# A fused attention and expert kernel: the fourth expert's first product on the second part by seven products of halves, and the float64 weights converted through DRAM

## The chip, the cores and the metric

The kernel runs on one core of a Trainium2 chip. The metric is the device time of one execution, in microseconds (us). Engines: PE multiplies matrices (PEld loads its weights), DVE and ACT work elementwise, POOL stands beside them, and SP issues the DMAs. Each engine runs its own instructions in order and waits for the others through semaphores.

## The reference

```python
x = attention(q, k, v)              # 2304 rows of 512
p = domain_probs / sum(domain_probs)
for e in range(4):                  # w1[e] 512 x 1024, w2[e] 1024 x 512
    h = maximum(x @ w1[e], 0)
    out += p[:, e] * (h @ w2[e])
h = out @ w_in                      # 512 x 1024, given as float64
ln = layernorm(h * softmax(h)) * g_ln
return ln @ w_out                   # 1024 x 512, given as float64
```

## The kernel before, in words

Every operand of a product is held as two float16 parts, a high and a low one, and every product is the sum of three: high by high, high by low, low by high. The 2304 rows are 18 tiles of 128. Tiles 0 to 5 are part 0 and tiles 6 to 17 are part 1; part 1 is four groups of three tiles (384 rows). A phase is one expert on one part: `j` 0 to 3 are the experts on part 0 (interleaved with the attention), `j` 4 to 7 the same experts on part 1. In the trace phases 6 and 7, the third and the fourth expert on part 1, stand from 685 to 802 us and from 802 to 928 us, and then the second layer follows (L1283 on).

A group of a phase has two halves. The **first product** is x by w1. In phases 4 and 7 it is the ordinary one (`phase_units`, `emit_h`): 8 column blocks of 12 matmuls of 384 columns, and for each block ACT writes the high part of relu(h) into a tile `hch` (L319) and DVE the low part (L320). In phases 5 and 6 it is made by seven products of halves (`st_phase`, `st_units`): x is cut into four quarters (two halves of its rows, two of the summed dimension), w1 likewise, and seven products of sums of quarters replace eight. The sums of x, `T`, are made once for each group (`t_steps`), those of w1, `S`, once for each expert and column half (`s_steps`, on DVE and ACT, in buffers `stf` and `stl`). A group has two column halves, each with seven products of 12 matmuls of 192 columns (L529). DVE joins their results: seven additions a column half (`add`, L541, tiles `stu`), which read the products from PSUM; ACT copies the first product (L559), and of each of four results ACT and DVE write high and low parts (L547, L548, two each). The products take turns in five PSUM banks, so PE can be at most five products ahead of the DVE addition that reads them.

The **second product**, `out_unit`, is 24 matmuls of 512 columns for each of the three tiles of a group (L331), and one DVE instruction adds it to `acc` (L355). For the last expert `finish_x2` scales, splits and transposes the finished tile for the second layer.

Weights: `next_w` hands out the steps of one matrix: four loads of 512 KB into `stage`, a scale, and four splits into the high and low parts `wt` (L263 on ACT, L266 on DVE). There is one `stage` buffer, so the next matrix can be loaded when the last L266 of the one before has read it. The two float64 matrices have another first step (`load64` and `to32`): 1024 KB are loaded, and seven DVE instructions on 1024 elements (L189 to L213) turn the two 32-bit words of a number into a float32 in `stage`. Before the change both matrices are converted so in phase 7.

`spread` puts such steps between the units of a phase, and a list scheduler of the framework then sets the order in which each engine gets its instructions; `high_priority` puts the evictions first. Memory comes from pools; a tile with one buffer (`bufs=1`) waits until the readers of the one before it are done, and a pool that takes the place of another waits for the readers of that.

Of the kernel before, what the change touches and what calls it, by code (L numbers as in the profile page):

```python
# [58 lines left out]
def tile_kernel(  # L59
# [101 lines left out]
    def w_steps(key, src, bits, inv, tag, load_eng, rows=None, hi_eng=None, place_raw="stage", known=False):  # L161
# [5 lines left out]
        wide = src.dtype == I64  # L167
        raw = {}

        def load64(c):  # L170
            def f():
                r = cv["pool"].tile([128, 1024, 2], I32, tag="raw64", name="raw64")
                dv = src.bitcast(I32).rearrange("(k p) f -> p k f", p=128)
                load_eng.dma_start(
                    out=r.rearrange("p (k f) w -> p k (f w)", k=q), in_=dv[:, c * q:(c + 1) * q]
                )
                raw[c] = r
            return f

        def to32(c):  # L180

            a = [None, None]

            def words():
                r = raw[c]
                a[0] = cv["pool"].tile([128, 1024], I32, tag="cvA", name="cvA")
                a[1] = cv["pool"].tile([128, 1024], I32, tag="cvP", name="cvP")
                h = r[:, :, 1]
                vec.tensor_scalar(  # L189
                    out=a[0], in0=h, scalar1=3, scalar2=0x3FFFFFF8,  # L190
                    op0=ALU.logical_shift_left, op1=ALU.bitwise_and,
                )
                vec.scalar_tensor_tensor(
                    out=a[0], in0=h, scalar=-0x40000000, in1=a[0], op0=ALU.bitwise_and, op1=ALU.bitwise_or
                )
                vec.tensor_scalar(
                    out=a[1], in0=h, scalar1=0x7FFFFFFF, scalar2=None, op0=ALU.bitwise_and
                )

            def value():  # L200
                top, tmp = a[0].bitcast(F32), a[1].bitcast(F32)
                vec.scalar_tensor_tensor(
                    out=top, in0=a[1], scalar=float(896 << 20), in1=top, op0=ALU.is_ge, op1=ALU.mult
                )
                vec.tensor_scalar(
                    out=a[1], in0=a[0], scalar1=-0x800000, scalar2=None, op0=ALU.bitwise_and
                )
                o = stage[key][:, c * 1024:(c + 1) * 1024]
                vec.scalar_tensor_tensor(
                    out=o, in0=raw.pop(c)[:, :, 0].bitcast(U32), scalar=2.0 ** -52, in1=tmp,  # L210
                    op0=ALU.mult, op1=ALU.mult,
                )
                vec.tensor_tensor(out=o, in0=o, in1=top, op=ALU.add)  # L213

            return [words, value]

# [59 lines left out]
        if wide:  # L276
            steps = [load64(0), load64(1), load]
            for c in range(4):
                steps += to32(c)
                if c < 2:  # L280
                    steps.append(load64(c + 2))
# [327 lines left out]
    def next_w(hi_eng=None, eng=None, place_raw="stage"):  # L609
# [4 lines left out]
        if i == 16:  # L614
            return w_steps("w_in", w_in, 15, inv, tag, eng)
# [816 lines left out]
```

## Time and profile before

| | us |
|---|---|
| median of 3 runs (lowest to highest) | 1121.17 (1119.93 to 1123.97) |
| the profiled execution | 1120.33 |
| its span | 1118.5 |
| PE busy in the span | 1054.0 |
| DVE busy in the span | 821.9 |
| ACT busy in the span | 500.8 |

The span lies within the profiled execution's time; 1.8 us lie around it. Matmuls overlap in the pipeline, as do instructions of DVE: what one costs its engine is the distance from its start to the next start, and not the duration that stands beside it.

### The profile page before, as it was taken

How to read it: one execution, taken by the hardware profiler on the slowest of the kernel's cores; microseconds unless marked ns; L12 is line 12 of the kernel's file. 1: busy time of each engine (PE TensorE's matmuls, PEld its weight loads, DVE VectorE, ACT ScalarE, POOL GpSimd, SP SyncE). 2: the span in 40 equal slices, each digit the busy share in tenths (PEclk: the TensorE clock that was granted, in tenths of full speed). 3: DMA queues.
4: the chain of work that ended last, by engine and by line, in shares of the span. 5: the costliest groups of instructions: out<-in, count | busy, mean ns of one | idle time of the engine just before them, and what ended most of it. 6: DMA issues, size and time to landing. Idle time of an engine off the chain costs nothing.

```text
span 1118.5 us, 19987 instructions
## 1 busy us (share of the span) xinstructions
PE 1054.0 (94%) x7776; PEld 642.1 (57%) x7776; DVE 821.9 (73%) x1818; ACT 500.8 (45%) x1115; POOL 184.7 (17%) x176
## 2 busy tenths in 40 slices
PE   4479889899998999999999999999999999999998
PEld 4456766466565555655567777766555554444443
DVE  6888787648678678536997459544999656999883
ACT  5657676647655457433542224211324332333222
POOL 4874632323115411000000000000000000000000
PEclk9999999899999999999999999999999999999999
DMA  9868986837648748332150002200422101443343
GB/s 306 236 149 176 248 183 148 246 94 209 174 103 236 152 114 224 74 43 56 33 203 6 1 1 79 73 1 1 148 87 96 38 19 29 89 90 85 76 85 85
DMA packets 216063, 125.87 MB, mean 113 GB/s; under 512 B 183712, under 2 KB 185760, under 8 KB 215456
## 3 DMA queue, kind: packets, MB, share of 16 engines
q1 hardware_dynamic: 215968, 124.59, 43.4%
q8 instruction: 61, 1.00, 0.4%
q14 instruction: 34, 0.28, 0.1%
HBM read 73.18 MB, written 6.29 MB: 71 GB/s over the span
## 4 chain that ended last, share of the span: by engine, by line
PE 73%; DVE 11%; DMA 8%; POOL 4%; issue 3%; ACT 1%; SPq 0%; DVEq 0%; ACTq 0%; POOLq 0%
PE ops L331 27%; PE hps L311 15%; PE hps L529 9%; PE h L1283 8%; PE o L1346 8%; DMA pT<-hl 6%; PE pv L872 3%; DVE wt L266 2%; DVE hl L843 1%; PE sps L799 1%; PE sps L800 1%; DVE stf L437 1%; DMA vraw<-in_vC_dram 1%; POOL wt L259 1%; DVE hch L320 1%
## 5 line engine op out<-in xcount | busy, mean ns | idle before, releaser
L331 PE MATMUL ops<-wt,hch 128*128 128x512 f16 x1728 | 387.6, 379 | 3.9 <-DVE wt L266 1.6
L331 PEld LDWEIGHTS <-hch 128*128 128x128 f16 x1728 | 166.2, 98 | 190.4 <-issue 4.4
L311 PE MATMUL hps<-xT,wt 128*128 128x384 f16 (+1 forms) x1920 | 268.5, 297 | 1.7 <-DVE hch L320 1.3
L311 PEld LDWEIGHTS <-wt 128*128 128x128 f16 x1920 | 164.0, 100 | 85.9 <-issue 4.0
L838 ACT ACTIVATE p<-sps,nm 128x320 f32<-128x320 f32 (+4 forms) x144 | 79.1, 553 | 89.9 <-DVE nm L809 59.6
L843 DVE TENSOR_TENSOR hl<-p,hl 128x320 f16<-128x320 f32 (+4 forms) x132 | 90.5, 699 | 33.2 <-ACT hl L842 32.9
L266 DVE SCALAR_TENSOR_TENSOR wt<-stage,ws,wt 128x1024 f16<-128x1024 f32 x72 | 99.7, 1392 | 8.3 <-ACT wt L263 6.9
L355 DVE SCALAR_TENSOR_TENSOR acc<-ops,coef,acc 128x512 f32<-128x512 f32 x54 | 40.4, 748 | 82.1 <-PE ops L331 82.1
L1283 PE MATMUL h<-wt,x2T 128*128 128x512 f16 x432 | 95.5, 379 | 0.8 <-DVE acc L355 0.8
L319 ACT ACTIVATE hch<-hps 128x384 f16<-128x384 f32 x130 | 62.3, 482 | 75.1 <-PE hps L311 74.6
L1346 PE MATMUL o<-wt,lt 128*128 128x512 f16 x432 | 95.5, 379 | 0.0
L320 DVE SCALAR_TENSOR_TENSOR hch<-hps,hch 128x384 f16<-128x384 f32 x130 | 70.5, 544 | 32.2 <-ACT hch L319 32.2
L799 PE MATMUL sps<-ks,qhi 128*128 128x288 f32 (+3 forms) x160 | 67.4, 424 | 23.7 <-ACT p L838 10.1
L263 ACT ACTIVATE wt<-stage,ws 128x1024 f16<-128x1024 f32 x64 | 71.1, 1140 | 6.0 <-PE hps L311 2.2
L1283 PEld LDWEIGHTS <-x2T 128*128 128x128 f16 x432 | 42.2, 98 | 52.0 <-issue 1.1
L541 DVE TENSOR_TENSOR stu<-stu,hps 128x384 f32<-128x384 f32 x112 | 59.4, 550 | 17.3 <-PE hps L529 17.3
L1346 PEld LDWEIGHTS <-lt 128*128 128x128 f16 x432 | 42.3, 98 | 50.9
L547 ACT ACTIVATE hch<-stu 128x192 f16<-128x192 f32 x128 | 39.2, 354 | 70.4 <-DVE stu L541 70.2
L842 ACT ACTIVATE hl<-p 128x320 f16<-128x320 f32 (+4 forms) x132 | 66.0, 522 | 7.3 <-DMA pT<-hl 6.7
L872 PE MATMUL pv<-v,pT 128*128 128x64 f16 x1392 | 54.8, 197 | 13.6 <-DMA pT<-hl 13.6
L529 PEld LDWEIGHTS <-S 128*128 128x128 f16 x768 | 64.3, 98 | 2.6
L872 PEld LDWEIGHTS <-pT 128*128 128x128 f16 x1392 | 49.4, 101 | 22.6 <-DMA pT<-hl 17.5
(155 smaller groups left out, 1366.7 us busy)
## 6 DMA issues: line engine op xcount, KB each, us to landing
stage<-in_w_dram SPq DMA_DIRECT2D x64, 512.0 KB, 5.9
raw<-in_qT_dram SPq DMA_DIRECT2D x34, 256.0 KB, 3.5
vraw<-in_vC_dram SPq DMA_DIRECT2D x30, 256.0 KB, 3.3
raw<-in_kT_dram SPq DMA_DIRECT2D x24, 288.0 KB, 3.5
raw<-in_w_in_dram SPq DMA_DIRECT2D x4, 1024.0 KB, 4.8
raw<-in_w_out_dram SPq DMA_DIRECT2D x4, 1024.0 KB, 5.0
out_dram<-o2s SPq DMA_DIRECT2D x16, 256.0 KB, 2.5
raw<-in_kT_dram SPq DMA_DIRECT2D x8, 192.0 KB, 4.1
```

Of the source, the lines that this page charges most:

```text
L263: h = bg_(act.activation(out=hi, in_=r, func=AF.Copy, scale=stage[key, "s"]), "A")
L266: stage["last"] = vec.scalar_tensor_tensor(out=lo, in0=r, scalar=stage[key, "s"], in1=hi, op0=ALU.mult, op1=ALU.subtract)
L311: pe.matmul(ps[:, j * n:j * n + n], w[:, a, kk, f * 128:(f + 1) * 128], x[:, b * KD + kk, c0:c0 + n], start=(m == 0), stop=(m == 3 * KD - 1),)
L320: nc.vector.scalar_tensor_tensor(out=h[:, 1, :n], in0=ps[:, :n], scalar=0.0, in1=h[:, 0, :n], op0=ALU.max, op1=ALU.subtract)
L331: pe.matmul(ps, hch[f][:, a, o0:o0 + 128], w[:, b, f, :], start=(m == 0), stop=(m == 3 * KF - 1))
L529: pe.matmul(ps[c][:, jj * HT:jj * HT + HT], lhs(a, kk, jj), rhs(b, kk), start=(m == 0), stop=(m == 5),)
L799: pe.matmul(o, hi[:, h % 4], rhs, start=True, stop=False)
L838: act.activation(out=dst, in_=src, func=AF.Exp, bias=nm[:, j + x:j + x + 1], scale=SCALE, accum_out=sums[:, h:h + 1],)
L843: anc["D"] = vec.tensor_tensor(out=hl[:, W + c0:W + c0 + n_], in0=pf[:, 0:n_], in1=hl[:, c0:c0 + n_], op=ALU.subtract)
L872: pe.matmul(o, tt[:, a * nch + c, :], v[:, bb, hs], start=(m == 0), stop=(m == total - 1))
L1283: pe.matmul(ps[:, half], x[:, a * KD + kk, c:c + 128], w[:, b, kk, half * 512:half * 512 + 512], start=(m == 0), stop=(m == 3 * KD - 1),)
L1346: pe.matmul(ps, tt[:, a * KF + f], w[:, b, f], start=(m == 0), stop=(m == 3 * KF - 1))
```

## The change

Phase 7 takes the form of phases 5 and 6: its first product is made by seven products of halves. For that its `S` is made at the end of phase 6, as that of phase 6 is made at the end of phase 5. The conversion of the float64 matrices is taken out of `w_steps`. It works on pieces of 512 elements, eight for each matrix: load the words (512 KB), seven DVE instructions, store the float32 piece (256 KB) to a DRAM tile `w32`. `w_in` is converted in phase 6 and `w_out` in phase 7, and then each is loaded from `w32` into `stage` as the other matrices are. The piece's DVE buffers `cvA` and `cvP` have one buffer each, its words two. The pool `tmp` of the sums and the pool `cv` of the conversion take each other's place (`swap`), and the tiles `stu` have a pool of their own with fewer buffers.

```diff
+    def to32_steps(src, tag):
+        n, W = src.shape[1], 512
+        d = dp.tile([src.shape[0], n], F32, tag=tag, name="w32")
...
+            def load():
+                a[2] = st_["cv"].tile([128, W, 2], I32, tag="raw64", name="raw64", bufs=2)
+                sync.dma_start(out=a[2].rearrange("p f w -> p (f w)"), in_=sv[:, k, 2 * f:2 * f + 2 * W])
+            def words():
+                a[0] = st_["cv"].tile([128, W], I32, tag="cvA", name="cvA")
+                a[1] = st_["cv"].tile([128, W], I32, tag="cvP", name="cvP")
...
+            def value():
...
+                vec.tensor_tensor(out=o, in0=o, in1=top, op=ALU.add)
+                sync.dma_start(out=dv[:, k, f:f + W], in_=o)
+            return [load, words, value]
...
+    def swap(name):
+        if "es" in st_:
+            st_["es"].close()
+        st_["es"] = ExitStack()
+        if name:
+            st_[name] = st_["es"].enter_context(tc.tile_pool(name=name, bufs=1))
...
         def add(k, x, y):
-            n = {"s": 3, "u": 2}.get(k[0], 1)
-            u[k] = st_["tmp"].tile([128, W], F32, tag=k[0] + str(n), name="stu", bufs=n)
+            n = 2 if k[0] == "s" else 1
+            u[k] = st_["acc"].tile([128, W], F32, tag=k[0] + str(n), name="stu", bufs=n)
...
-    for j in (5, 6):
+    for j in (5, 6, 7):
...
+        if j < 7:
...
+            end = [s_steps(e + 1, h) for h in range(2)]
...
+        elif j == 6:
+            swap("cv")
+            st = to32(0)
+            n = len(st) // 3
+            tasks = [tasks[0] + st[:n], tasks[1] + st[n:2 * n], st[2 * n:], pb + [lambda: swap("tmp")]]
+        else:
+            swap("cv")
+            st = to32(1)
+            n = len(st) // 2
+            pa, qa = next_w()
+            pb, qb = next_w()
+            tasks = [post + st[:n] + pa[:5], st[n:] + pa[5:] + qa, pb[:5], (pb[5:], qb)]
...
-    us = phase_units(7, GROUPS[1], psb)
```

Two places on DVE. The lines of the changed file are others: there the additions are L556, the low parts L563, the weight splits L216, the additions to `acc` L362, the conversion L251 to L274 and the scaling of rows of `w_out` L186.

First, DVE at the start of phase 6, behind the last addition to `acc` of phase 5. Before:

```order
L266 SCALAR_TENSOR_TENSOR wt_9521<-stage_9268,ws_9270,wt_9521 128x1024
L541 TENSOR_TENSOR stu_9125<-stu_9109,hps_9112 128x384
L541 TENSOR_TENSOR stu_9131<-stu_9075,hps_9112 128x384
L266 SCALAR_TENSOR_TENSOR wt_9521<-stage_9268,ws_9270,wt_9521 128x1024
L541 TENSOR_TENSOR stu_9146<-stu_9109,hps_9133 128x384
L266 SCALAR_TENSOR_TENSOR wt_9521<-stage_9268,ws_9270,wt_9521 128x1024
L548 SCALAR_TENSOR_TENSOR hch_9045<-stu_9125,hch_9045 128x192
L541 TENSOR_TENSOR stu_9167<-stu_9131,hps_9154 128x384
```

The same place in the changed kernel, DVE:

```order
L556 TENSOR_TENSOR stu_9158<-stu_9118,hps_9145 128x384
L216 SCALAR_TENSOR_TENSOR wt_9498<-stage_9187,ws_9189,wt_9498 128x1024
L251 TENSOR_SCALAR cvA_9307<-raw64_9263 128x512
L258 TENSOR_SCALAR cvP_9308<-raw64_9263 128x512
L216 SCALAR_TENSOR_TENSOR wt_9498<-stage_9187,ws_9189,wt_9498 128x1024
L563 SCALAR_TENSOR_TENSOR hch_9053<-stu_9135,hch_9053 128x192
L563 SCALAR_TENSOR_TENSOR hch_9054<-stu_9135,hch_9054 128x192
L563 SCALAR_TENSOR_TENSOR hch_9053<-stu_9158,hch_9053 128x192
L563 SCALAR_TENSOR_TENSOR hch_9054<-stu_9158,hch_9054 128x192
L255 SCALAR_TENSOR_TENSOR cvA_9307<-raw64_9263,cvA_9307 128x512
L216 SCALAR_TENSOR_TENSOR wt_9498<-stage_9187,ws_9189,wt_9498 128x1024
L556 TENSOR_TENSOR stu_9224<-stu_9208,hps_9211 128x384
```

Behind it come `stu_9181<-stu_9141,hps_9168`, which is what `stu_9167<-stu_9131,hps_9154` is before, and the fourth split. Three conversion instructions and three more low parts have moved ahead of it.

Second, DVE in phase 7 between the second products of its second group and the first product of its third, where the rows of `w_out` are scaled by `g_ln`. Before:

```order
L213 TENSOR_TENSOR stage_10865<-stage_10865,cvA_10988 128x1024
L236 TENSOR_SCALAR stage_10865<-stage_10865,gl_94 128x512 x4
L189 TENSOR_SCALAR cvA_11031<-raw64_10950 128x1024
L196 TENSOR_SCALAR cvP_11032<-raw64_10950 128x1024
L355 SCALAR_TENSOR_TENSOR acc_6808<-ops_10868,coef_10576,acc_6808 128x512
L193 SCALAR_TENSOR_TENSOR cvA_11031<-raw64_10950,cvA_11031 128x1024
```

The same place in the changed kernel, DVE:

```order
L216 SCALAR_TENSOR_TENSOR wt_11318<-stage_10878,ws_10880,wt_11318 128x1024
L362 SCALAR_TENSOR_TENSOR acc_6808<-ops_11319,coef_10881,acc_6808 128x512
L264 SCALAR_TENSOR_TENSOR cvA_11123<-cvP_11124,cvA_11123 128x512
L362 SCALAR_TENSOR_TENSOR acc_6852<-ops_11358,coef_10881,acc_6852 128x512
L267 TENSOR_SCALAR cvP_11124<-cvA_11123 128x512
L131 TENSOR_SCALAR x2i_95<-xt_11345 128x1
L270 SCALAR_TENSOR_TENSOR cvP_11124<-raw64_11054,cvP_11124 128x512
L135 TENSOR_SCALAR x2i_95<-x2i_95 128x1
L186 TENSOR_SCALAR stage_11525<-stage_11525,gl_94 128x512
L131 TENSOR_SCALAR x2i_95<-xt_11384 128x1
L186 TENSOR_SCALAR stage_11525<-stage_11525,gl_94 128x512
L274 TENSOR_TENSOR cvP_11124<-cvP_11124,cvA_11123 128x512
```

The last split of `w_in` (the first row) has moved close ahead of the first L186, whose `stage` now comes by a load that may begin only when that split has read the buffer; before, DVE itself had written it.

## Rows read from the trace of the kernel before

**Rows 1.** PE timeline, groups of phases 6 and 7: start, us, engine, line.
```profile
743.56 1.15 PE L529 MATMUL hps<-xT,wt 128*128 128x192 f16 x12
...
757.42 15.70 PE L331 MATMUL ops<-wt,hch 128*128 128x512 f16 x72
...
802.36 15.76 PE L311 MATMUL hps<-xT,wt 128*128 128x384 f16 x96
817.96 15.70 PE L331 MATMUL ops<-wt,hch 128*128 128x512 f16 x72
```

**Rows 2.** All instructions of line 529: duration ns min/median/max.
```profile
L529 PEld LDWEIGHTS <-S x768: 97/98/98, 542.6 to 786.7; 128*128 128x128 f16 x192
```

**Rows 3.** Windows: length, busy us of PE, PEld, DVE, ACT, POOL; clock, DMA.
```profile
685.00:802.00 117.00, 117.00 (x933) 81.53 (x932) 73.34 (x154) 31.98 (x81) 0.00 (x0) 1.00 0.13 47
802.00:928.00 126.00, 125.35 (x679) 66.26 (x678) 94.67 (x167) 47.42 (x89) 0.00 (x0) 1.00 0.25 73
```

**Rows 4.** DVE timeline, start of phase 6 and a stretch of phase 7.
```profile
687.26 0.74 DVE L355 SCALAR_TENSOR_TENSOR acc<-ops,coef,acc 128x512 f32<-128x512 f32 x1
687.92 0.62 DVE L548 SCALAR_TENSOR_TENSOR hch<-stu,hch 128x192 f16<-128x192 f32 x2
688.46 0.69 DVE L425 TENSOR_TENSOR S<-stf,S 128x512 f16<-128x512 f32 x1
689.06 0.75 DVE L355 SCALAR_TENSOR_TENSOR acc<-ops,coef,acc 128x512 f32<-128x512 f32 x1
...
695.43 0.55 DVE L541 TENSOR_TENSOR stu<-stu,hps 128x384 f32<-128x384 f32 x1
695.90 0.35 DVE L548 SCALAR_TENSOR_TENSOR hch<-stu,hch 128x192 f16<-128x192 f32 x1
696.16 1.28 DVE L266 SCALAR_TENSOR_TENSOR wt<-stage,ws,wt 128x1024 f16<-128x1024 f32 x1
697.36 0.55 DVE L541 TENSOR_TENSOR stu<-stu,hps 128x384 f32<-128x384 f32 x1
...
808.97 0.68 DVE L189 TENSOR_SCALAR cvA<-raw 128x1024 int32<-128x1024 int32 x1
809.57 0.69 DVE L196 TENSOR_SCALAR cvP<-raw 128x1024 int32<-128x1024 int32 x1
...
810.64 1.21 DVE L193 SCALAR_TENSOR_TENSOR cvA<-raw,cvA 128x1024 int32<-128x1024 int32 x1
811.78 0.54 DVE L320 SCALAR_TENSOR_TENSOR hch<-hps,hch 128x384 f16<-128x384 f32 x1
...
875.23 0.48 DVE L236 TENSOR_SCALAR stage<-stage,gl 128x512 f32<-128x512 f32 x1
875.62 0.15 DVE L135 TENSOR_SCALAR x2i<-x2i 128x1 f32<-128x1 f32 x1
```

**Rows 5.** PE timeline, the first products of phase 6.
```profile
695.95 2.14 PE L529 MATMUL hps<-T,S 128*128 128x192 f16 x24
```

**Rows 6.** DMA issues by line: KB each, median us from issue to landing.
```profile
spill<-acc SPq DMA_DIRECT2D x6, 256.0 KB, 2.0
```

**Rows 7.** DMAs into `stage` from 685 to 702 us: four in a row.
```profile
DMA to landing us min/median/max: 4.2/5.6/6.5
```

**Rows 8.** PE timeline: its waits, in brackets what ended them.
```profile
122.42 1.78 PE L872 MATMUL pv<-v,pT 128*128 128x64 f16 x30 [2.24 <-DMA pT<-hl]
580.45 1.15 PE L529 MATMUL hps<-T,wt 128*128 128x192 f16 x12 [1.62 <-DVE stu L541]
928.20 2.10 PE L1283 MATMUL h<-wt,x2T 128*128 128x512 f16 x9 [0.84 <-DVE acc L355]
```

**Rows 9.** Windows at the first and the second of these waits, same columns as above.
```profile
120.00:133.10 13.10, 10.86 (x109) 7.58 (x106) 7.49 (x14) 8.35 (x19) 6.72 (x7) 0.87 1.04 243
...
123.00:124.00 1.00, 1.00 (x23) 1.00 (x21) 0.00 (x0) 0.87 (x3) 0.82 (x2) 0.50 0.97 323
...
568.00:626.00 58.00, 56.23 (x447) 38.83 (x446) 40.47 (x88) 17.34 (x44) 0.00 (x0) 1.00 0.19 69
```

More of the change, by code (lines that the diff above doesn't have):

```diff
@@ L165, in w_steps @@
         q = k // 4
[L167 to L215, printed above, removed]
         def load():
@@ L275, in w_steps @@
         steps = [load] + [load_part(c) for c in range(4)]
[L276 to L281, printed above, removed]
         if rows is not None:
@@ L286, in w_steps, with piece @@
         return steps, [place] + [split(c) for c in range(4)]
+    def to32_steps(src, tag):
+        n, W = src.shape[1], 512
+        d = dp.tile([src.shape[0], n], F32, tag=tag, name="w32")
+        sv = src.bitcast(I32).rearrange("(k p) f -> p k f", p=128)
+        dv = d.rearrange("(k p) f -> p k f", p=128)
+        steps = []
+        def piece(k, f):
+            a = [None, None, None]
+            def load():
[4 more added lines that the diff above has]
+                a[1] = st_["cv"].tile([128, W], I32, tag="cvP", name="cvP")
+                h = a[2][:, :, 1]
+                vec.tensor_scalar(
+                    out=a[0], in0=h, scalar1=3, scalar2=0x3FFFFFF8,
+                    op0=ALU.logical_shift_left, op1=ALU.bitwise_and,
+                )
+                vec.scalar_tensor_tensor(
+                    out=a[0], in0=h, scalar=-0x40000000, in1=a[0], op0=ALU.bitwise_and, op1=ALU.bitwise_or
+                )
+                vec.tensor_scalar(
+                    out=a[1], in0=h, scalar1=0x7FFFFFFF, scalar2=None, op0=ALU.bitwise_and
+                )
+            def value():
+                top, o = a[0].bitcast(F32), a[1].bitcast(F32)
+                vec.scalar_tensor_tensor(
+                    out=top, in0=a[1], scalar=float(896 << 20), in1=top, op0=ALU.is_ge, op1=ALU.mult
+                )
+                vec.tensor_scalar(
+                    out=a[1], in0=a[0], scalar1=-0x800000, scalar2=None, op0=ALU.bitwise_and
+                )
+                vec.scalar_tensor_tensor(
+                    out=o, in0=a[2][:, :, 0].bitcast(U32), scalar=2.0 ** -52, in1=o,
+                    op0=ALU.mult, op1=ALU.mult,
+                )
+                vec.tensor_tensor(out=o, in0=o, in1=top, op=ALU.add)
+                sync.dma_start(out=dv[:, k, f:f + W], in_=o)
+            return [load, words, value]
+        ps = [piece(k, f) for k in range(src.shape[0] // 128) for f in range(0, n, W)]
+        steps = [ps[0].pop(0)]
+        for a, b in zip(ps, ps[1:] + [[]]):
+            steps += b[:1] + a
+            del b[:1]
+        return d, steps
@@ L289, in tile_kernel, with to32 @@
+    last_w = [w_in, w_out]
+    def to32(i):
+        if last_w[i].dtype != I64:
+            return []
+        last_w[i], steps = to32_steps(last_w[i], f"w32{i}")
+        return steps
     xT, x2T, acc = {}, {}, {}
@@ L556, in f1 @@
             product(1, A(0, 0), B(0, 0))
-            u["b"] = st_["tmp"].tile([128, W], F32, tag="b1", name="stu", bufs=1)
+            u["b"] = st_["acc"].tile([128, W], F32, tag="b1", name="stu", bufs=1)
             with tc.high_priority(offset=PRI):
@@ L601, in st_phase @@
             else:
-                gs = spread(gs + outs, (1, n + 3, tasks[g]))
+                if isinstance(tasks[g], tuple):
+                    gs = spread(gs + outs, (1, n, tasks[g][0]), (n + 0.2, n + 2.5, tasks[g][1]))
+                else:
+                    gs = spread(gs + outs, (1, n + 2.5, tasks[g]))
             us += gs
@@ L614, in next_w @@
         if i == 16:
-            return w_steps("w_in", w_in, 15, inv, tag, eng)
+            return w_steps("w_in", last_w[0], 15, inv, tag, eng)
         if i == 17:
-            return w_steps("w_out", w_out, 15, inv, tag, eng, rows=gl)
+            return w_steps("w_out", last_w[1], 15, inv, tag, eng, rows=gl)
         j, second = divmod(i, 2)
@@ L1227, in tile_kernel @@
     st_["keep"] = sts.enter_context(tc.tile_pool(name="keep", bufs=1))
-    st_["tmp"] = sts.enter_context(tc.tile_pool(name="tmp", bufs=2))
+    st_["acc"] = sts.enter_context(tc.tile_pool(name="sacc", bufs=1))
+    swap("tmp")
     moe.reverse()
```

25 lines of the change are left out of this document (8 added, 17 removed).

## The prediction

> **What bounds the kernel now.** I read the PE timeline of phases 6 and 7 first. A group of phase 6 spends 757.42 − 743.56 = 13.86 us on its first product and a group of phase 7 spends 817.96 − 802.36 = 15.60 us; the second product, 72 matmuls, follows without a gap in both [rows 1]. The reader should see that the two kinds of group differ in the first product alone. The windows come next: in phases 6 and 7 PE is busy for 117.00 of 117 and 125.35 of 126 us at a clock of 1.00 (2.4 GHz), DVE for 73.34 and 94.67 us, ACT for 31.98 and 47.42 us [rows 3]. So PE sets the time there, and the engine to watch is DVE, because the change gives it work. The third view is DVE's own timeline, for what an instruction costs it: the distance between two starts, not the duration beside it [rows 4].
>
> **What PE saves.** Four groups of phase 7 take the form of phase 6: 4 × (15.60 − 13.86) = 6.96 us less, if PE doesn't wait. A matmul of 192 columns then costs 13.86 / 168 = 82.5 ns, one of 384 columns 15.60 / 96 = 162.5 ns. The form has 168 weight loads a group in place of 96, each recorded with 98 ns [rows 2], and yet the matmuls start 82.5 ns apart: the loads overlap. The Trainium skill speaks against the form here (TensorE: Matmul & The Clock Gate, LDWEIGHTS): a weight load takes its columns divided by 1.2, in ns. By that, as an estimate, 128 columns need 107 ns, a group would take 168 × 0.107 = 17.9 us, and the change would cost 9 us where the rows give a gain of 7. The trace has this very instruction stream in phase 6 and differs from it, and the trace decides.
>
> **What DVE gets.** Prices from start to start [rows 4]: an addition of 384 elements 695.90 − 695.43 = 0.47 us; a low part (687.92 to 688.46, two of them) 0.27; 512 elements of two tensors 0.60 (688.46 to 689.06); an addition to `acc` 0.66; a weight split 1.20; a TENSOR_SCALAR of 1024 elements 0.60 and the three-operand form 1.14 (810.64 to 811.78); a scaled row of `stage` 0.39. For 512 elements of the conversion the trace has no row. I bound a TENSOR_SCALAR by half of 0.60 and by the 0.39 of the scaled row and take 0.35; I bound the three-operand form by 0.60 and 0.66 and take 0.63.
> - Phase 7: 56 additions × 0.47 + 64 low parts × 0.27 = 43.6 us, in place of 32 × 0.47 = 15.0 us for L320: +28.6 us.
> - `S` of the fourth expert: 14 instructions a half, 28 × 0.60 = +16.8 us, in phase 6.
> - Conversion: a piece is 3 × 0.35 + 3 × 0.63 + 0.60 = 3.5 us, sixteen are 57 us. Before, eight of 3 × 0.60 + 4 × 1.14 = 6.4 us are 51 us: +6 us.
>
> Together 51 us on DVE in phases 6 and 7, whose 168 us busy become about 219 of 236 us. On the average it fits, with 17 us to spare; so the question is where it doesn't fit for a moment. PE can run ahead of DVE's additions by five products, some 5 us, and during a second product (15.5 us) DVE owes it little. A wait arises where a backlog larger than this stands at the start of a group. ACT has room: it writes as many high parts as DVE low ones, and even at DVE's 0.27 us each its 47 us grow by 17, of 126. The 28 more DMAs move 8 MB more in phases whose DMA share is 0.13 and 0.25 [rows 3]: bandwidth is no bound, what counts is the time to landing and who stands in line.
>
> **Place A, start of phase 6.** Behind the last `acc` addition of phase 5 the order has, up to the end of the addition `stu_9181` that frees the bank PE wants: 0.66, three additions 1.41, three splits 3.60, two L251/L258 0.70, four low parts 1.08, L255 0.63, an addition 0.47 and the last with its full 0.55: 9.1 us. PE meanwhile has two matmuls, six products and five matmuls of 512 columns: 0.17 + 5.94 + 1.08 = 7.2 us. DVE starts some 0.2 us behind PE's last matmul, so PE waits 2.0 us. The same sum before is 6.9 us from 689.06 and gives 695.96; the trace has the end at 695.43 + 0.55 = 695.98 [rows 4], and PE wanted the bank at 695.95 + 0.99 = 696.94 [rows 5]: no wait, 1 us to spare. Behind the waiting PE nothing else can go. Bounds 1.0 (if a split and an addition less stand in the way) and 2.5; I take **2.0**.
>
> **Place B, end of phase 6.** The pool `cv` takes `tmp`'s place, so the words of the first piece of `w_out` load only when the last `S` is written. DVE's first L251 waits for them, and behind it stands the addition `stu_10702` whose bank PE wants two matmuls and six products (6.1 us) after the last second product. No row has this load; by size the nearest is a 512 KB load into `stage`, which lands after 4.2 to 6.5 us, median 5.6 of four in a row [rows 7]. Then come 0.35 + 0.27 + 0.35 + 0.55 = 1.5 us. So PE waits 0 at 4.2, 1.0 at 5.6, 1.9 at 6.5. It is the first of two loads, so nearer the low end; the last `S` may be late behind ACT's squares. I take **0.5**.
>
> **Place C, third group of phase 7.** (Sums by the prices above.) The rows of `w_out` are now loaded, and that load may begin only when the last split of `w_in` has read `stage`. In the second group DVE has 6.6 us of additions, 3.8 us of low parts, 0.66 us of L402, 4.9 us of conversion and 0.6 us of small ones: 16.5 us against PE's 13.86, so it enters the second product 2.6 us late. It then needs 8.9 us to the end of that split: 11.7 us into a second product of 15.5 us. The load lands 4.2 us later, and DVE, with 3.1 us of work before L186, waits 1.1 us. From the landing to the end of `stu_11560`, whose bank PE wants, I count 3.5 us to the group's first addition and 10.3 us behind it; another 0.5 us for the second pair of L186, whose load waits for two stores. Sum: 11.7 + 4.2 + 13.8 + 0.5 = 30.2 us. PE wants it after 15.5 us of second product, eleven products (10.9 us) and six matmuls of 512 columns (1.3 us): 27.7 us. It waits **2.5** us. Bounds: 0 if DVE isn't behind in the group before, 4.8 if the load takes 6.5 us.
>
> **The rest.** In the conversion the next L258 waits until the store of the piece before it has landed, 2.0 us for 256 KB by the spill [rows 6]. DVE has 0.35 to 1.6 us of other rows between; the waits (some 0.4 to 1 us each) lie mostly in second products, which hide them: there DVE has only three `acc` additions to give. The Trainium skill has for this store (DMA: Bandwidth & Descriptors, Anatomy of one DMA) a fixed 2.0 us, most of it the receipt of the write, plus the bytes: 2.6 us as an estimate. The row says 2.0; with 2.6 place C would cost 0.6 us more. The wait of 1.62 us at 580.45 [rows 8] lies before the changed phases; its order moves by a few rows only, so I leave it, bounds −1.6 to +1. The second layer's first wait, 0.84 us [rows 8], is for the last `acc` addition and stays; its second product needs `w_out` only 30 us later.
>
> **Sum.** −6.96 + 2.0 + 0.5 + 2.5 = −2.0 us. Against the profiled execution's 1120.33 that is 1118.4; its time lies 0.84 below the median of the runs, so the forecast for the median is **1119.2 us**, no change that a measurement of this kernel can tell (about 0.5%, 5.6 us).
>
> **Rivals.** (1) DVE doesn't hold PE up at all: 1121.17 − 6.96 = 1114.2 us, faster by 0.6%. For it: five banks of slack, and phase 6 before had no wait. Against it: the sum at A, whose counterpart met the trace to 0.02 us. It decides where all waits together stay under 1.4 us. Chance 0.13.
> (2) Slower: DVE at the head of a DMA's landing. If loads land at 6.5 us and not at 4.2, C is 4.8 and B 1.9, A stays 2.0; and each PE wait over 2 us may take the clock with it. The trace has that: PE waited 2.24 us up to 122.42 [rows 8], and from 123 to 124 the granted clock stood at 0.50 (1.2 GHz); over 13.1 us it was 0.87 in the mean, a loss of 13.1 × 0.13 = 1.7 us [rows 9]. After the wait of 1.62 us it stayed at 1.00 [rows 9]. Three places, three falls: 8.7 + 5.1 − 6.96 = +6.8, 1128.0 us. It decides where waits and falls reach 12.6 us together. Against it: the landings are at the upper end only with four loads in a row. Chance 0.12.
> (3) The halves don't run at phase 6's pace because `S` is late: its second half is written about when the group begins and wanted four products later, a spare of 3 us. If late by as much again, +3 us: 1122 us. Chance 0.05.
>
> **How the numbers follow.** The forecast has 0.70, and with rival 3 "same" has 0.75; faster 0.13, slower 0.12. The range reaches down to rival 1's 1114.2 and up to the upper bounds of all three places with two falls of the clock, −6.96 + 2.5 + 1.9 + 4.8 + 3.4 = +5.6, 1126.8; what lies outside is half of rival 1 and most of rival 2, 0.17.
>
> **What would show it.** Right: in phase 7 twelve matmuls of 192 columns every 0.99 us; PE waits of some 2 us for an addition in the first group of phase 6, and of 2 to 3 us in the third of phase 7; DVE waits for `raw64` at B and for `stage` at C; the second layer starts near 926 us instead of 928.20. Wrong: PE without waits in phases 6 and 7 (then rival 1), waits in every group, or a clock under 1.00 there (rival 2).

## The result and the profile after

| | median of the runs, us | ratio to the kernel before, 95% interval |
|---|---|---|
| before | 1120.96 (1119.74 to 1123.97, 8 runs) | |
| changed | 1127.30 (1124.11 to 1129.13, 8 runs) | 1.0051 [1.0034, 1.0068] |

The change makes the kernel slower, by 5.7 us [3.8, 7.6], about 0.5%. The forecast was 1119.2 us and the range ended at 1126.8: the result lies 0.5 us above it. Two later comparisons on other occasions gave 1.0024 [1.0008, 1.0040] and 1.0048 [1.0029, 1.0066]; all three say slower.

The profiled execution of the changed kernel took 1129.13 us (span 1127.0). The windows of phases 6 and 7, with the columns of [rows 3]:

```profile
685.00:802.00 117.00, 112.70 (x900) 80.58 (x899) 99.42 (x211) 32.93 (x82) 0.00 (x0) 0.97 0.25 84
802.00:928.00 126.00, 122.25 (x979) 85.26 (x978) 113.16 (x275) 55.50 (x132) 0.00 (x0) 1.00 0.35 103
```

Before, PE had no idle time in the first of these windows and 0.65 us in the second; now it is idle for 4.3 and 3.75 us, and in the first its clock isn't full. PE's waits are listed by who ends them (us in total, times, the longest), from 500 us to the end. L544 is the first product's matmuls in the changed file, L338 the second product's, L1305 the second layer's, L574 ACT's copy of the first product:

```profile
PE hps L544 <- DVE stu L556: 6.2, 9, 3.0
PE hps L544 <- ACT stu L574: 1.3, 2, 1.1
PE h L1305 <- DVE acc L362: 0.8, 1, 0.8
PE ops L338 <- DVE hch L563: 0.5, 1, 0.5
```

The long one stands in phase 6, in its third group. PE's timeline there:

```profile
752.06 1.15 PE L544 MATMUL hps<-T,wt 128*128 128x192 f16 x12
753.81 1.15 PE L544 MATMUL hps<-xT,S 128*128 128x192 f16 x12 [0.60 <-DVE stu L556]
758.01 2.08 PE L544 MATMUL hps<-xT,wt 128*128 128x192 f16 x12 [3.05 <-DVE stu L556]
759.88 2.13 PE L544 MATMUL hps<-T,S 128*128 128x192 f16 x12
761.80 2.03 PE L544 MATMUL hps<-xT,wt 128*128 128x192 f16 x12
763.67 2.14 PE L544 MATMUL hps<-T,S 128*128 128x192 f16 x24
```

Two things are to be seen. PE waits 0.60 and 3.05 us for an addition. And the three products behind the long wait start 1.87, 1.92 and 1.87 us apart, where a product of twelve such matmuls takes 0.99 us at full clock: 2.7 us more. The granted clock (the last column but two) says why:

```profile
753.00:757.00 4.00, 1.36 (x15) 1.07 (x13) 1.39 (x4) 0.00 (x0) 0.00 (x0) 0.97 0.42 150
757.00:764.00 7.00, 5.99 (x41) 5.71 (x41) 7.00 (x18) 2.84 (x9) 0.00 (x0) 0.53 0.10 37
764.00:770.00 6.00, 6.00 (x57) 4.71 (x56) 6.00 (x17) 1.23 (x4) 0.00 (x0) 1.00 0.01 3
```

The mean from 757 to 764 is 0.53, close to the lower level, 1.2 GHz. What held the addition stands in DVE's timeline:

```profile
750.16 0.69 DVE L270 SCALAR_TENSOR_TENSOR cvP<-raw,cvP 128x512 f32<-128x512 uint32 x1
750.89 0.69 DVE L274 TENSOR_TENSOR cvP<-cvP,cvA 128x512 f32<-128x512 f32 x1
751.61 0.43 DVE L251 TENSOR_SCALAR cvA<-raw 128x512 int32<-128x512 int32 x1
...
753.22 0.55 DVE L556 TENSOR_TENSOR stu<-stu,hps 128x384 f32<-128x384 f32 x1
756.34 0.43 DVE L258 TENSOR_SCALAR cvP<-raw 128x512 int32<-128x512 int32 x1 [2.58 <-DMA w<-cvP]
756.80 0.69 DVE L264 SCALAR_TENSOR_TENSOR cvA<-cvP,cvA 128x512 f32<-128x512 int32 x1
757.41 0.55 DVE L556 TENSOR_TENSOR stu<-stu,hps 128x384 f32<-128x384 f32 x1
```

L274 finishes a piece in `cvP` at 751.58 and the store of it follows. L258 of the next piece writes `cvP`, of which there is one, so it stands at the head of DVE's queue until the store has landed (its data are written and the semaphore tells so), 2.58 us idle. The addition that PE needs is two rows behind it and ends at 757.96; PE goes on at 758.01. Over phase 6 and over phase 7, DVE's largest waits are:

```profile
DVE cvP L258 <- DMA w<-cvP: 10.7, 5, 2.6
...
DVE cvP L258 <- DMA w<-cvP: 3.5, 3, 1.7
DVE x2i L131 <- ACT xh L127: 2.7, 5, 0.8
DVE stage L186 <- DMA stage<-w: 2.2, 2, 1.3
```

Why a store takes so long is seen in the queue of SyncE (SP) and in the landing times. SyncE:

```profile
743.58 0.33 SPq L89 DMA_DIRECT2D raw<-in_w_in_dram  x1
744.31 0.33 SPq L89 DMA_DIRECT2D w<-cvP  x1
750.88 0.33 SPq L89 DMA_DIRECT2D raw<-in_w_in_dram  x1
751.61 0.33 SPq L89 DMA_DIRECT2D w<-cvP  x1
```

A load of 512 KB is issued 0.73 us ahead of each of these two stores of 256 KB: its buffer comes free with L270, one instruction before the piece is done. Three stores, each with its issue and under it its time to landing:

```profile
L89 SPq DMA_DIRECT2D w<-cvP x1: 326/326/326, 751.6 to 751.6; - x1
DMA to landing us min/median/max: 4.7/4.7/4.7
...
L89 SPq DMA_DIRECT2D w<-cvP x1: 326/326/326, 727.1 to 727.1; - x1
DMA to landing us min/median/max: 2.5/2.5/2.5
...
L89 SPq DMA_DIRECT2D w<-cvP x1: 333/333/333, 877.8 to 877.8; - x1
DMA to landing us min/median/max: 2.0/2.0/2.0
```

The load ahead of them was issued 0.7, 2.1 and 2.5 us earlier. Of all sixteen stores, six that were issued 0.7 us or less behind a load took 3.7 to 4.7 us, two that were 1.1 and 1.3 us behind one 2.8 and 3.5 us, seven that were 1.6 us or more behind one 2.0 to 2.5 us; the sixteenth was 1.6 us behind its load too, but that one followed four loads into `stage`, and it took 4.8 us.

The trace of the kernel before has such stores too, under the median of [rows 6]. Of its six spills of 256 KB four had nothing in flight and landed after 1.96 to 2.01 us. The other two were issued at 564.09 us, 0.47 us behind the last of four loads into `stage`, and at 569.10 us, with two of these loads and the first store still in flight:

```profile
DMA to landing us min/median/max: 7.5/7.5/7.5
...
DMA to landing us min/median/max: 3.1/3.1/3.1
```

At the start of phase 7 the halves do what was forecast: from the second product at 767.63 to that at 826.43, over the last group of phase 6 and the first of phase 7, it is 58.80 us, twice a group of phase 6; before it was 817.96 − 757.42 = 60.54 [rows 1], 1.74 us more. But the second group waits 0.24 + 0.65 + 0.42 us behind two of L258's waits, and the third 2.43 us in five pieces, of which the longest:

```profile
885.55 0.39 PE L338 MATMUL ops<-wt,hch 128*128 128x512 f16 x1 [0.52 <-DVE hch L563]
886.99 1.15 PE L544 MATMUL hps<-xT,wt 128*128 128x192 f16 x12 [1.05 <-ACT stu L574]
...
936.75 3.61 PE L1305 MATMUL h<-wt,x2T 128*128 128x512 f16 x16 [0.84 <-DVE acc L362]
```

The second layer starts at 936.75 instead of 928.20 [rows 8].

**Where the 8.5 us of the two spans lie.** Four marks of PE's timeline cut it: the second products that start at 552.41, 610.42 and 757.42 in the kernel before, and the start of the second layer. The table gives how much longer each stretch is than in the kernel before (58.01, 147.00 and 170.78 us there), for the changed kernel and for the kernels of the next section; behind the last mark all agree to 0.5 us.

| kernel | ahead of 552 | 552 to 610 (phase 5) | 610 to 757 (to third group of phase 6) | 757 to 928 (phase 7) |
|---|---|---|---|---|
| changed | +4.45 | −1.95 | +7.71 | −1.66 |
| changed, second profile (e5) | +4.38 | −1.94 | +6.72 | −1.31 |
| changed, third profile (e10) | +3.97 | −1.94 | +5.96 | −1.37 |
| e1 store from the pair buffer | +2.57 | −1.95 | +0.33 | −3.14 |
| e2 load behind store | +3.66 | −1.95 | 0.00 | −5.49 |
| e9 the same again | −0.37 | −1.94 | 0.00 | −4.63 |
| e6 the same in phase 6 alone | +0.70 | −1.94 | 0.00 | +0.52 |
| e8 the same in phase 7 alone | +4.63 | −1.94 | +7.52 | −4.07 |
| e3 no conversion | −0.53 | −1.94 | 0.00 | −6.22 |
| e4 conversion moved alone | −0.19 | −1.95 | +7.50 | +1.07 |
| e7 load on GpSimd's queue | +1.32 | −1.94 | +4.93 | +1.06 |

The first column is nearly all code that no kernel here changes: PE's order is the same in all of them up to 523 us, where the difference already stands. It varies by 5 us from execution to execution; e2 and e9 are the same kernel and lie at +3.66 and −0.37. The changed kernel's three profiles all lie near +4, but e6, which has their order on PE throughout and differs from them only from phase 6 on, lies at +0.70. It is no effect of the change that these profiles can show, and it is why two single spans may not be compared. The three stretches that the change touches give +4.1, +3.5 and +2.7 us for the changed kernel, against +5.7, +2.7 and +5.4 by the three ratios. In the first profile the 7.71 are four waits, 0.45 + 0.21 + 0.60 + 3.05 us, some 0.16 us beside each (the overlap with the matmul before, which a wait also loses), and 2.7 us of low clock.

### The profile page after: what moved, and what is told of

It is laid out like the page before. It is cut to its first block, busy times and chain, and to the rows that moved or that the text cites. A ratio compares the mean times of both kernels' runs of the same rounds, so it can differ in the third digit from the quotient of the medians.

```text
span 1127.0 us, 20900 instructions
## 1 busy us (share of the span) xinstructions
PE 1054.1 (94%) x8064; PEld 662.6 (59%) x8064; DVE 867.3 (77%) x1990; ACT 512.5 (45%) x1163; POOL 183.5 (16%) x176
## 4 chain that ended last, share of the span: by engine, by line
PE 65%; DMA 15%; DVE 11%; POOL 4%; issue 3%; ACT 1%; SPq 0%; ACTq 0%; POOLq 0%; DVEq 0%
PE ops L338 23%; PE hps L318 10%; PE hps L544 9%; PE h L1305 8%; PE o L1368 8%; DMA pT<-hl 8%; DMA w<-cvP 3%; PE pv L890 3%; DVE stu L556 2%; PE sps L817 2%; DVE wt L216 1%; DVE hch L563 1%; DMA vraw<-in_vC_dram 1%; PE sps L818 1%; POOL ks L698 1%
## 5 line engine op out<-in xcount | busy, mean ns | idle before, releaser
L338 PE MATMUL ops<-wt,hch 128*128 128x512 f16 x1728 | 390.8, 380 | 4.2 <-DVE wt L216 1.6
L338 PEld LDWEIGHTS <-hch 128*128 128x128 f16 x1728 | 166.2, 98 | 187.1 <-issue 5.3
L318 PE MATMUL hps<-xT,wt 128*128 128x384 f16 (+1 forms) x1536 | 205.9, 289 | 1.8 <-DVE hch L327 1.4
L318 PEld LDWEIGHTS <-wt 128*128 128x128 f16 x1536 | 125.8, 99 | 62.2 <-issue 5.9
L562 ACT ACTIVATE hch<-stu 128x192 f16<-128x192 f32 x192 | 58.7, 354 | 132.4 <-DVE stu L556 132.4
L216 DVE SCALAR_TENSOR_TENSOR wt<-stage,ws,wt 128x1024 f16<-128x1024 f32 x72 | 98.6, 1376 | 8.9 <-ACT wt L213 7.6
L544 PEld LDWEIGHTS <-S 128*128 128x128 f16 x1152 | 97.7, 98 | 7.8 <-issue 2.3
L556 DVE TENSOR_TENSOR stu<-stu,hps 128x384 f32<-128x384 f32 x168 | 89.0, 553 | 9.6 <-PE hps L544 9.6
L1305 PE MATMUL h<-wt,x2T 128*128 128x512 f16 x432 | 95.5, 379 | 0.8 <-DVE acc L362 0.8
L544 PE MATMUL hps<-T,S 128*128 128x192 f16 x864 | 82.9, 248 | 0.4 <-DVE stu L556 0.4
L544 PEld LDWEIGHTS <-wt 128*128 128x128 f16 x864 | 74.4, 99 | 13.1 <-issue 5.8
L362 DVE SCALAR_TENSOR_TENSOR acc<-ops,coef,acc 128x512 f32<-128x512 f32 x54 | 40.4, 748 | 47.1 <-PE ops L338 46.8
L1305 PEld LDWEIGHTS <-x2T 128*128 128x128 f16 x432 | 42.3, 98 | 52.0 <-issue 1.1
L327 DVE SCALAR_TENSOR_TENSOR hch<-hps,hch 128x384 f16<-128x384 f32 (+1 forms) x98 | 52.9, 543 | 19.9 <-ACT hch L326 19.9
```

What stands on the lines that cost most here:

```text
L216: stage["last"] = vec.scalar_tensor_tensor(out=lo, in0=r, scalar=stage[key, "s"], in1=hi, op0=ALU.mult, op1=ALU.subtract)
L318: pe.matmul(ps[:, j * n:j * n + n], w[:, a, kk, f * 128:(f + 1) * 128], x[:, b * KD + kk, c0:c0 + n], start=(m == 0), stop=(m == 3 * KD - 1),)
L338: pe.matmul(ps, hch[f][:, a, o0:o0 + 128], w[:, b, f, :], start=(m == 0), stop=(m == 3 * KF - 1))
L544: pe.matmul(ps[c][:, jj * HT:jj * HT + HT], lhs(a, kk, jj), rhs(b, kk), start=(m == 0), stop=(m == 5),)
L1305: pe.matmul(ps[:, half], x[:, a * KD + kk, c:c + 128], w[:, b, kk, half * 512:half * 512 + 512], start=(m == 0), stop=(m == 3 * KD - 1),)
```

## The experiments

The texts of this section also call PE TensorE, DVE VectorE, ACT ScalarE, POOL GpSimd and SP SyncE. Of the low clock the expectations count 3.4 us, half of 6.8; PE stood still for a part of these, so the products lost 2.7.

Theory "store": VectorE at the head of its queue, waiting for the store of the piece before, delays the additions; the long wait takes the clock along. Rivals: "volume" (51 us more on VectorE are too much by themselves), "halves" (the new form of phase 7 doesn't give what phase 6's did), and, for the store's landing, "queue order" against "shared engines".

**e1: the piece is stored from the buffer of its word pairs.**

```diff
-                vec.tensor_tensor(out=o, in0=o, in1=top, op=ALU.add)
-                sync.dma_start(out=dv[:, k, f:f + W], in_=o)
+                vec.tensor_tensor(out=a[2].rearrange("p f w -> p (f w)")[:, :W].bitcast(F32), in0=o, in1=top, op=ALU.add)
+                sync.dma_start(out=dv[:, k, f:f + W], in_=a[2].rearrange("p f w -> p (f w)")[:, :W].bitcast(F32))
```

> The changed kernel, but L274 writes the finished float32 piece into the first half of its own buffer of word pairs (raw64, two of them) and the store reads it there; cvP is free as soon as L274 has run. Nothing of the computation is left out. Theory 'store' (VectorE stood at L258 until the store of the piece before had landed: 10.7 us in five waits in phase 6 of the profiled execution, the sums of L556 behind it, TensorE behind these for 0.45 + 0.21 + 0.60 + 3.05 us, and a clock of 0.5 for 6.8 us, which costs 3.4 us): no wait of L258 on a store is left, TensorE's waits in phase 6 are under 1 us together, its clock stays at 1.00 there, and the median goes from 1127.3 to about 1120 (1117.5 to 1121.5). Theory 'volume' (the 56 and 64 more conversion instructions of phases 6 and 7 by themselves delay the sums, and the store wait only fell into the same time): the waits in phase 6 stay at 3 us and more and the median is 1125 to 1129.

Measured: 1116.32 us median, ratio 0.9946 [0.9926, 0.9966], so 11.8 us less than the changed kernel by the ratios (0.9946 against 1.0051), more than "store" had said (1117.5 to 1121.5), since phase 7 gained too. No wait of L258 on a store is left, phase 6 costs 0.33 us, the clock stays at 1.00 from 500 us to the second layer. "Volume" falls: the same sixteen pieces are converted.

**e2: the load is issued behind the store.**

```diff
-                sync.dma_start(out=a[2]..., in_=sv[:, k, 2 * f:2 * f + 2 * W])
+                ld = sync.dma_start(out=a[2]..., in_=sv[:, k, 2 * f:2 * f + 2 * W])
+                stores and after(ld, stores[-1])
...
-                sync.dma_start(out=dv[:, k, f:f + W], in_=o)
+                stores.append(sync.dma_start(out=dv[:, k, f:f + W], in_=o))
```

> The changed kernel, but the load of word pairs that takes over a piece's buffer is issued on the DMA queue behind the store of that piece, not ahead of it; cvP stays a single buffer. Nothing of the computation is left out. Theory 'store behind a load' (a 256 KB store lands 4.0 to 4.8 us after its issue where a 512 KB load was issued 0.7 us ahead of it, 2.4 to 2.8 us where the load was 1.2 to 2.1 us ahead, 2.0 us where there was none): the stores land in 2.0 to 2.5 us throughout, VectorE's waits at L258 fall from 14.2 us in phases 6 and 7 to under 4 us, the longest PE wait of phase 6 is under 1.5 us, the median is 1118 to 1122. If a store's landing doesn't hang on the load ahead of it, landings stay at 3 to 4.8 us, the waits stay, and the median is 1125 to 1129.

Measured: 1115.19 us median, ratio 0.9947 [0.9930, 0.9963]. The median lies under the 1118 to 1122 that was written down; phase 7 gained about 4 us beside what phase 6 gave. `cvP` is still one buffer; only two DMAs are meant to change places. The windows, L258's waits in phase 6, and the landing of the phase's stores:

```profile
685.00:802.00 117.00, 117.00 (x956) 83.08 (x954) 106.99 (x224) 35.40 (x88) 0.00 (x0) 1.00 0.27 88
802.00:928.00 126.00, 124.30 (x968) 84.81 (x967) 111.82 (x276) 57.23 (x133) 0.00 (x0) 1.00 0.34 102
```

```profile
DVE cvP L258 <- DMA w<-cvP: 3.2, 4, 1.5
```

```profile
DMA to landing us min/median/max: 2.0/2.3/3.9
```

DVE is busy for 107 and 112 us, more in the first window than in the changed kernel because the work isn't pushed out of it, and PE doesn't wait once in phase 6. The median landing falls from 4.1 us (2.5 to 4.8 in the changed kernel from 700 to 760 us) to 2.3; the one of 3.9 follows directly behind the four loads into `stage`. The loads now follow some 0.4 us behind the stores, so a load issued behind a store doesn't hold it up. In phase 7 seven of the eight stores land after 2.0 to 2.4 us and one after 3.4. L258's waits fall from 14.2 us to 4.3 in both phases, a little over the 4 that were written down. The list scheduler places other instructions a little differently for e1 and e2 too, so the gain isn't the two DMAs' alone by proof; e6, where PE's order doesn't change, closes most of that gap.

**e3: no conversion.**

```diff
-    last_w = [w_in, w_out]
+    last_w = [w1[0], w2[0]]
```

> The changed kernel without the conversion: the last layer takes expert 0's two float32 weights (same shapes) in place of its own, so its result is another one, and no pieces, stores or word pairs are left; all else, the first product from products of halves in phase 7 too, is as in the changed kernel. If the halves give what the rows of the other experts say (4 groups x 1.74 us = 7.0 us) and only the conversion gave it back: 1113 to 1115.5, phase 7's first products 13.86 us each, TensorE waits in phases 6 and 7 under 1.5 us together. If the halves themselves give less in phase 7, because VectorE or ScalarE can't follow: 1117 to 1121, with waits in phase 7 of 2 us and more.

Measured: 1115.50 us median, ratio 0.9939 [0.9916, 0.9962], 6.8 us less than before: the halves are worth about what the rows said, and with the load behind the store all but about 1 us of it is reached. The kernel before, too, has the conversion that is left out here, but PE idles only 0.65 us in its phase 7 [rows 3], so leaving it out there could give little. The 1117 us of two runs lie above the expectation of 1113 to 1115.5, the profile's phase 7 is −6.22 where −6.96 was counted.

**e4: the conversion moved, phase 7 in the ordinary way.** The end of the diff; `plain` deals the units of `phase_units` to the same four groups of tasks; the fourth expert's `S` isn't made.

```diff
-        for _, u, _ in st_phase(e, psb, psh, tasks, end):
+        us = st_phase(e, psb, psh, tasks, end) if j < 7 else plain(7, psb, tasks)
+        for _, u, _ in us:
```

> The changed kernel's conversion (small pieces through DRAM in phases 6 and 7), but phase 7's first product in the ordinary way as before the change; nothing of the computation is left out. Theory 'store': phase 6 is that of the changed kernel up to its third group, with PE waits of 3 to 4.5 us and a fall of the clock worth 3.4 us, phase 7 has no waits that matter (its first products write no sums on VectorE), so 1121 + 4 to 8 = 1125 to 1129, slower than the kernel before and about as slow as the changed one. Theory 'halves' (it is phase 7's sums beside the conversion that cost the time): 1119 to 1122.

Measured: 1129.24 us median, ratio 1.0068 [1.0045, 1.0091]. The theory "store" said 1125 to 1129, and the median lies 0.2 us above that. The long wait and the slow products behind it are there again, 2.65 us (its lines have other numbers, L556 for L544, L568 for L556):

```profile
749.22 1.15 PE L556 MATMUL hps<-xT,S 128*128 128x192 f16 x12 [0.59 <-DVE stu L568]
753.01 2.08 PE L556 MATMUL hps<-xT,wt 128*128 128x192 f16 x12 [2.65 <-DVE stu L568]
754.88 2.13 PE L556 MATMUL hps<-T,S 128*128 128x192 f16 x12
756.80 2.13 PE L556 MATMUL hps<-xT,wt 128*128 128x192 f16 x12
```

So the move alone costs 7.6 us by the ratio; by the marks +7.50 in phase 6, +1.07 behind it and −1.95 in phase 5. The halves then take back some 2.5 us in phase 7 (+1.07 against −1.45 in the mean of the changed kernel's three profiles), not 7; that their sums meet the same stores there fits e8 (−4.07 with these loads behind the stores). "Halves" falls as the cause of the loss.

**e6 and e8: load behind store in one phase only.** As e2, with `tag == "w320"` (phase 6) or `tag == "w321"` (phase 7) added to the condition. In e6 the order on PE is that of the changed kernel, instruction for instruction; on DVE and ACT some change places from phase 6 on.

> The changed kernel with the load put behind the store for the pieces of w_in alone (phase 6); w_out's pieces in phase 7 stay as changed, and TensorE's order of instructions is that of the changed kernel. Nothing of the computation is left out. Theory 'both phases' (phase 6 cost 4.3 us of PE waits and 3.4 us of clock, phase 7 some 3.7 us of PE waits): phase 6 shows no wait over 1 us and a clock of 1.00, phase 7 keeps 3 to 4 us of waits, and the time is between the two: the changed kernel's less 7.7, 1119 to 1121.5 where before is 1121 (ratio 0.998 to 1.000). Theory 'phase 6 alone' (all that load-behind-store gave came from phase 6, and phase 7 follows when it isn't late): 1114.5 to 1117 (ratio 0.994 to 0.9965), phase 7 with under 1.5 us of waits.

> The counterpart of the run with phase 6 alone: the load is put behind the store for the pieces of w_out (phase 7), w_in's pieces in phase 6 stay as changed. Nothing of the computation is left out. Theory 'both phases': phase 6 keeps its PE waits (4.2 us in four, the longest about 3) and its fall of the clock, phase 7's waits go from 3.7 us to under 1.5 us, and the time is the changed kernel's less 4 us (3 to 6), about 1123 where the changed kernel has 1127. Theory 'phase 6 alone': phase 7 gains nothing once phase 6 is late, 1126 to 1128.

Measured: e6 1119.76 us, 0.9961 [0.9946, 0.9975], beside the changed kernel's 1126.83 (e5), 7.1 us less. e8 1123.93 us, 1.0008 [0.9993, 1.0024], beside 1128.46 (e10), 4.5 us less. "Both phases" holds: 7.1 + 4.5 = 11.6 us, and the two together (e9, beside the same 1128.46) give 13.1 by the medians, 12.3 by the ratios. e6's ratio to before lies under the 0.998 to 1.000 that was written down and in the range of "phase 6 alone" (0.994 to 0.9965); the changed kernel itself stood at 1.0024 in that comparison and not at 1.0051. The profiles and e8 decide: in e6's, phase 7 keeps its waits, eight of 5.8 us together (3 to 4 were expected), the longest 1.70 us, and is 0.52 us longer than before the change. In e8's, phase 6 keeps its waits, and those of phase 7 are 1.8 us together, where under 1.5 was expected.

```profile
839.45 1.15 PE L544 MATMUL hps<-xT,wt 128*128 128x192 f16 x12 [1.70 <-DVE stu L556]
```

**e5, e9 and e10: the changed kernel twice more, and e2 again.**

> The changed kernel itself once more, for the same chip's runs of before and for a second profile. Its phase 6 should again show the long PE wait of about 3 us behind L556 and a clock of 0.5 for some 6.8 us right behind it; the fall of the clock for 6.8 us near 429 us, which the first profile of it shows ahead of the code that differs and none of the four experiments shows, should be gone if it belongs to that execution alone, and be there again if the changed kernel brings it. Median 1124 to 1129, ratio 1.003 to 1.007.

> The kernel with the load behind the store in both phases once more, to stand on one chip beside the changed kernel and the one with phase 7 alone. Sum of the parts by the landmarks of TensorE's timeline (7.7 us in phase 6, 3.8 us in phase 7): the changed kernel less 11.5 us, 1114 to 1117, and 0.993 to 0.996 of the kernel before.

> The changed kernel beside these two on the same chip: 1125 to 1129, 1.002 to 1.006 of the kernel before. Its third profile also tells whether the fall of the clock near 430 us, in code that the change leaves alone, comes with this kernel each time (two of two so far, none of six others).

Measured: e5 1126.83 us, 1.0024 [1.0008, 1.0040], its ratio just under the range; e10 1128.46 us, 1.0048 [1.0029, 1.0066]; e9 1115.32 us, 0.9938 [0.9916, 0.9960]. Phase 6's long wait comes each time (3.42 and 2.66 us), and a low clock behind it, for about half as long as in the first profile. The fall of the clock near 430 us is in e5 and e8 too, but not in e10, so it doesn't come with the changed kernel each time. It follows a wait of the attention's matmuls for a transposing DMA, here in the first profile of the changed kernel; in e10 the longest such wait there is 0.8 us:

```profile
427.20 0.70 PE L890 MATMUL pv<-v,pT 128*128 128x64 f16 x18 [1.29 <-DMA pT<-hl]
429.63 1.14 PE L890 MATMUL pv<-v,pT 128*128 128x64 f16 x18 [1.74 <-DMA pT<-hl]
```

What makes that wait long in some executions was not looked for.

**e7: the loads on GpSimd's queue.**

```diff
-                sync.dma_start(out=a[2].rearrange("p f w -> p (f w)"), in_=sv[:, k, 2 * f:2 * f + 2 * W])
+                gp.dma_start(out=a[2].rearrange("p f w -> p (f w)"), in_=sv[:, k, 2 * f:2 * f + 2 * W])
```

> The changed kernel with the loads of word pairs issued by GpSimd, which has no work in phases 6 and 7, on its own DMA queue, the stores still on SyncE's; nothing of the computation is left out. Theory 'queue order' (a store waits because it stands behind the load in one queue): stores land in 2.0 to 2.5 us even where a load was issued just ahead, VectorE's waits at L258 are under 3 us, 1114 to 1119. Theory 'shared engines' (load and store are moved by the same 16 DMA engines, whichever queue they come from): stores issued within 1 us of a load still take 3.5 to 4.8 us, the waits at L258 stay at 8 us and more, 1122 to 1129.

Measured: 1125.14 us, 1.0020 [1.0006, 1.0035]. The stores from 680 to 760 us, issued 0.5 to 1.8 us behind a load, land no sooner from a queue of their own, and VectorE waits for them as long (its idle time in front of L258, and the time to landing):

```profile
  DMA w<-cvP: 11.1, 5
...
DMA to landing us min/median/max: 3.0/4.1/4.9
```

"Queue order" falls, "shared engines" holds: what counts is that the load is in flight when the store is issued, not that it stands ahead of it in a queue. The Trainium skill has the rule (DMA: Bandwidth & Descriptors, Issuing engines are not separate DMA queues): DMAs issued by ScalarE, SyncE or GpSimd run on the same 16 DMA engines and interleave there. These rows agree, but no run here tells the DMA engines from the DRAM behind them as the place where load and store meet.

e1, e2 and e9 beat both kernels, by 0.5 to 0.6% the one before and by 1.0 to 1.1% the changed one; the change was worth 6 to 7 us once its stores were out of the way.

## Why the prediction was wrong

Step by step, in the order of the prediction; the measured sums are of the changed kernel's profiles, the marks of the table.

1. **What PE saves: right.** −6.96 us counted; the same weight loads and the same 13.86 us a group appear in phase 7, and without the conversion (e3) that stretch is 6.22 us shorter and the kernel 6.8 us faster. The row was worth more than the estimate from the Trainium skill (TensorE: Matmul & The Clock Gate, LDWEIGHTS) that spoke against it.
2. **What DVE gets: right in sum.** 168 to about 219 us busy was forecast; e2, where nothing is pushed out of the windows, has 107.0 + 111.8 = 218.8. A piece alone was too cheap: without other rows between, five of its seven instructions take 3.10 us (748.51 to 751.61) and the first two 0.45 + 0.61 (744.86 to 745.92), 4.2 us and not 3.5. The change adds 32 DMAs (40 for 8) and not 28; nothing hangs on that.
3. **Place A, 2.0 us: absent.** DVE's 9.1 us were right (from 692.25 to 701.26, 9.0). But `hps_9265` doesn't want that addition's bank: in the order it waits for ScalarE alone, and the first product that waits for DVE is the next one, a product and seven matmuls of 512 columns later, at 701.73. The wait was hung on the wrong product.
4. **Place B, 0.5 us: absent.** The first load landed 3.3 us after its issue, under the 4.2 to 6.5 of [rows 7]; DVE waited 0.77 us at L251, PE not at all. The bounds began at 0.
5. **Place C, 2.5 us: 2.43 us in the profile,** but that the size agrees is in good part luck. The last split of `w_in` ends 14.4 us into the second product, not 11.7 (its own terms, 2.6 + 8.9, make 11.5). DVE waits 2.2 us for the load into `stage` at L186 there, and 2.5 us in e2, where the store's waits are short; yet PE loses only 0.70 us in e2. So most of C seems to have come from the same cause as the rest, DVE late behind stores; PE's order differs a little in e2's phase 7, so this is argued and not shown. The bound of 0 "if DVE isn't behind" had it.
6. **The rest, the step that failed.** L258's wait was there, word for word: "the next L258 waits until the store of the piece before it has landed, 2.0 us for 256 KB by the spill". But it was priced at 0.4 to 1 us, "mostly in second products, which hide them", and stands in the sum with nothing. The 2.0 us of [rows 6] is the median of six, and four of these had nothing ahead of them; the other two, 7.5 and 3.1 us, lay in the same group. The load that is issued ahead of a store was not looked at: the prediction counted bandwidth ("is no bound") and not what is in flight. The estimate of 2.6 us beside it, from the Trainium skill (DMA: Bandwidth & Descriptors, Anatomy of one DMA), goes by a fit for DMAs issued by GpSimd, and SyncE issues this store; alone such stores took 2.0 us, and behind a load more than either. With 2.0 us, from 751.61, L258 at 753.7 would have waited for nothing and the addition would have ended near 755.3, for a PE that wanted it near 755.0. With 4.7 us it ended at 757.96. So the waits were not 0.4 to 1 us but up to 2.6, 14.2 us in eight, and the longest stood ahead of an addition in a first product, not beside a second one. This is +6.0 to +7.7 us in phase 6 and some 3 of the 5.5 us that phase 7 lost of its 7.
7. **The wait of 1.62 us at 580.45** was left in the sum and is gone: the stretch is 1.95 us shorter in every changed kernel. Its additions stand between the weight splits in another order now; that this is why was not tried.
8. **Rival 2** came nearest: 1128.0 us, DVE at the head of a DMA's landing, waits over 2 us that take the clock along. Its mechanism was right in kind and its place wrong: it spoke of loads at B and C, and the time is near its 1128.0 partly by luck. The price of a fall was 1.7 us there and 2.7 us here. It had 0.12.

Against the forecast's −2.0 us: phase 5 −1.95, A −2.0, B −0.5, phase 6 +6.8 (mean of three profiles), phase 7 +3.0 (−1.45 in place of −6.96 + 2.5) make +5.35, so +3.4 us, where the three ratios give +5.7, +2.7 and +5.4. +3.4 lies in the second and the third interval and 0.4 us under the first; what is left over is within the spread of the code ahead, and no run settles it.

## What to carry to other kernels

When an in-order engine gets work that writes a single buffer which a DMA then reads, price the wait at the next write by the landing time under the DMAs that are in flight then, not by a median (the slowest of the six spills would have shown it), and look for what stands behind that instruction: a wait of 2.6 us on VectorE cost TensorE 3.05 us and 2.7 us more of low clock. Here a store that someone waits for belonged ahead of a load that nobody waited for yet, and the load's buffer came free just too early; making the load follow the store gave 12 us, another queue some 2. Cut timelines at common marks before two spans are subtracted.

## What the hardware showed that was not expected

- A 256 KB store lands 2.0 us after its issue alone and 3.7 to 4.7 us where a 512 KB load was issued up to 0.7 us ahead of it from the same queue; with the loads on GpSimd's queue, 0.5 to 1.8 us ahead, it was 3.0 to 4.9 us (e7), and behind four loads in a row 7.5 us (before).
- Waits of TensorE of 1.95 us (e7, phase 7), 2.65, 2.66, 2.66, 3.05 and 3.42 us were each followed by a granted clock of 0.5; after 1.51 (e7), 1.62 [rows 8, 9] and 1.70 us (e6) it stayed at 1.00. Near 430 us 1.74 and 1.78 us (the changed kernel, e8 and e5), each with a shorter wait 2.5 us ahead of it, were followed by 0.5 too.
- On VectorE an instruction that needs the result of the one just before it starts 0.12 to 0.13 us later than one that doesn't: the 512-element TENSOR_SCALAR 0.46 us to the next start (748.51 to 748.97) against 0.34 (695.50 to 695.84), the three-operand form 0.73 (748.97 to 749.70) against 0.60 (870.11 to 870.71).
- Code that is the same in all these kernels took up to 5 us more or less. Falls of the clock behind the attention's waits for DMAs are a part of it: from 420 to 440 us the mean granted clock was 0.83 in the changed kernel's first profile and 1.00 before the change. How large a part was not measured.
